# Softmax reciprocals loaded, applied and mixed earlier in the first steps of an attention and feed-forward kernel

## The chip, the core and the metric

The kernel runs on one core of a Trainium2 chip. The metric is the device time of one launch in microseconds (us). Before the change the median of three runs is 909.43 us (909.01 to 910.25).

## What is computed

Softcapped attention for 8 batches of 12 heads (448 positions, 64 wide), and a gated channel mixing on its output, all in float32:

```python
scores = cap * np.tanh(scale * q @ k.T / cap)          # cap 30, scale 1/8
attn = exp(scores - max) / (sum + 1e-9)
x = (attn @ v)                                          # 8 x 448 x 768 over all heads
x_prev = x shifted by one position
xk = mu_k * x + (1 - mu_k) * x_prev
xr = mu_r * x + (1 - mu_r) * x_prev
v = np.maximum(xk @ w_k, 0.0) ** 2 @ w_v
out = v / (1 + exp(-(xr @ w_r)))
```

## The kernel before

Two heads of a batch are a pair; there are 48 pairs, and the program is a row of steps i = 0, 1, 2, ..., one per pair, software-pipelined over several steps. Each step is written as a string of operation names (`STEP_0` for steps 0 to 5, `STEP_6`, `STEP_7`, then `EVEN_6` and `ODD_6` in turn for steps 8 to 13, and `EVEN` and `ODD` behind them), and the loop in `step` issues the operations in the order of the string. That order is the order on each engine; engines meet only through semaphores. No scheduler reorders anything.

What step i does for which pair:

- `S0` to `S3`: TensorE computes the scores of pair i, transposed (keys on the partitions), into PSUM (tile `s`, two buffers). `tanh` and `exp` (L265, L278, ScalarE) turn them into `p`. Operands are split into a high and a low float32r part, so each score product takes three matmuls.
- `red` (L308, VectorE): sums of exponentials of pair i into `r1`; `gather` (L314, four DMAs on SyncE's queue) brings those of pair i-1 to 32 partitions; `recip` (L318 to L325, four small VectorE instructions) makes their reciprocals; `rec_store` (L328) writes them to DRAM and `rec_load` (L337, two DMAs into the one buffer `r`) reads them back, broadcast to 64 partitions each. `rec_load` takes the last stored ones: in steps 2 to 6 it stands at a step's start and reads what the step before stored (pair i-2); from step 6 on a `rec_load` stands at the step's end, right behind `rec_store` and `load_qk` of the same step.
- `V` (L289, L299): TensorE multiplies values by `p` of pair i-1 into PSUM tile `pv` (two buffers). `norm` (L341, VectorE) multiplies `pv` of pair i-2 by `r` into `x`; `mix_old` (L351, ScalarE) and `mix_new` (L356, VectorE) form `xk`, and `mix_old` writes over `pv`. So `pv` of pair i-2 is free for `V` of pair i only when `mix_new` of pair i-2 has read it. `x_high` and `x_low` (GpSimd) split `xk` for the matmuls.
- `K` (L430): parts of the key matmul of the batch before, from the last part of step 6 on; `relu` and `k_store` take its results away.
- The weights arrive as 64-bit numbers and are taken apart on the way: one piece is loaded per step (`weight_load`, L463, 384 KB at first, 768 KB in steps 5 to 8, whose issue stands behind `gather` and `load_v`), `weight_abs` (ScalarE), five VectorE instructions issued by `f` (L499 to L508), `weight_sum` (GpSimd: sum L515 and high part L100). For the four 768 KB pieces the low part is a subtraction of its own, `weight_low` (L531, an instruction of L110), at the start of the next step on VectorE: `lo = sq - hi`.

All DMAs named here are issued by SyncE in program order, and one that waits holds up those behind it.

Of the kernel before, what the change touches and what calls it, by code (L numbers as in the profile page):

```python
# [60 lines left out]
K exp2 red2 weight_rest weight_sum relu k_store prep K prep K relu k_store prep  # L61
weight_abs load_qk rec_load quad_load tail_open weight_store"""
EVEN = ODD.replace("V S2", "V S3 S2").replace(" red3", "").replace("tanh2", "tanh3 tanh2").replace("K relu k_store prep\n", "K exp3 red3 relu k_store prep\n")
STEP_0 = """gather rec_load load_v x_store weight_load S0 S1 V0 S2 V1 S3 V2 V3 f f f f f tanh0 exp0 red0
weight_sum tanh1 exp1 weight_abs red1 recip rec_store qk_high qk_low tanh2 exp2 norm red2 tanh3 exp3 mix_old red3 mix_new x_high x_low
load_qk weight_store"""
ODD_6 = """load_v gather weight_load weight_low S0 S1 V S2 red3 f f f f f gate_new tanh0 exp0 red0 norm
weight_sum tanh1 exp1 K relu_early red1 tanh2 qk_rise relu exp2 mix_old k_store mix_new recip x_store rec_store qk_low x_high x_low gate_old
K red2 weight_rest weight_sum relu k_store K K weight_abs relu k_store load_qk rec_load weight_store"""
EVEN_6 = ODD_6.replace("V S2", "V S3 S2").replace(" red3", "").replace("tanh2 qk_rise", "tanh3 tanh2 qk_high").replace("weight_abs", "weight_abs exp3 red3")  # L70
STEP_6 = """gather rec_load load_v x_store weight_load weight_low S0 S1 V0 S2 V1 S3 V2 V3 f f f f f tanh0 exp0 red0
weight_sum tanh1 exp1 red1 recip rec_store tanh2 qk_rise exp2 norm red2 K K K K qk_low weight_abs tanh3 exp3 mix_old red3 mix_new x_high x_low
load_qk rec_load"""
STEP_7 = """gather load_v x_store weight_load weight_low S0 S1 V S2 f f f f f tanh0 exp0 red0 norm
weight_sum tanh1 exp1 K relu_early red1 tanh2 qk_rise relu exp2 mix_old k_store mix_new recip rec_store qk_low x_high x_low gate_old
# [6 lines left out]
def f(ap):  # L82
    return ap.bitcast(F32)


class Body:
# [440 lines left out]
                self.w_done.append((n, sq))  # L527
        self.w_sum = []

    def weight_low(self):  # L530
        for lo, sq, hi in self.w_low:  # L531
            self.sub("v", lo, sq, f(hi))
        self.w_low = []

    def weight_store(self):
        for n, sq in self.w_done:
            c, h = divmod(n - NWK, 2)
            self.nc.sync.dma_start(self.w_d[c, :, h * HC:(h + 1) * HC], sq)
        self.w_done = []
# [218 lines left out]
    def step(self, i, KS):  # L758
# [8 lines left out]
        pair.update(x_store=i - 3, gate_new=i - 3)  # L767
        for op in ((STEP_0, STEP_0) if i < 6 else (STEP_6, STEP_7) if i < ALONE else (EVEN_6, ODD_6) if i < REST[0] else (LAST, LAST) if NPAIR <= i < NPAIR + 2 else (EVEN, ODD))[i % 2].split():
            j = pair.get(op)
# [221 lines left out]
```

## Time and profile before

| | |
|---|---|
| median of 3 runs | 909.43 us |
| the profiled execution | 910.17 us, of which 908.4 us span from its first to its last instruction |
| busy, of the span | TensorE 97%, VectorE 80%, ScalarE 69%, GpSimd 45% |
| granted TensorE clock, mean | 0.997 |
| DMA | 170.03 MB, mean 187 GB/s |

The span divides into the attention steps and the two large products behind them. Steps are told apart here by the first tanh of each on ScalarE: step 2 begins at 21.22 us, step 3 at 31.04, step 4 at 40.27, step 5 at 48.66, step 6 at 57.00, step 7 at 68.11. TensorE is less than fully busy in the first 69 us and nearly without a gap behind that.

### The profile page before, as it was taken

The page shows a single profiled execution, that of the slowest core. Times are in us where ns is not written, and L with a number is a line of the kernel's source. Part 1 is how long each engine was busy: PE and PEld are TensorE (multiplying, and loading weights), DVE is VectorE, ACT ScalarE, POOL GpSimd, SP SyncE. Part 2 cuts the span into 40 slices and gives each one's busy share as a digit, 9 for nine tenths or more (in the row PEclk, how much of TensorE's full clock was granted, in tenths as well). Part 3 has the DMA queues.
Part 4 walks back from the last instruction along what each step waited for, and adds up shares of the span by engine and source line. Part 5 has one row for each costly group of instructions (what it writes and reads, how often), then busy time and mean ns, then how long its engine had stood idle before and what let it go on. Part 6 is the DMA issues. An engine that isn't in the chain of part 4 may idle for free.

```text
span 908.4 us, 15218 instructions
## 1 busy us (share of the span) xinstructions
PE 879.3 (97%) x5034; PEld 693.1 (76%) x5034; DVE 729.7 (80%) x1246; ACT 628.9 (69%) x907; POOL 411.0 (45%) x345
## 2 busy tenths in 40 slices
PE   6789999999999999999999999999999999999996
PEld 2236666666666666666666789999999999999996
DVE  6888996988988898888868857787887667877775
ACT  8888887887878887878877475556565535555553
POOL 5896584776776776776764200000000023443330
PEclk9999999999999999999999999999999999999999
DMA  5476746776766766666565455745445546777673
GB/s 166 152 212 185 213 153 196 198 203 190 210 191 198 220 195 203 197 199 197 173 197 178 161 190 179 233 149 170 151 154 166 169 149 189 219 219 218 217 219 108
DMA packets 123672, 170.03 MB, mean 187 GB/s; under 512 B 22592, under 2 KB 107712, under 8 KB 123584
## 3 DMA queue, kind: packets, MB, share of 16 engines
q1 hardware_dynamic: 114224, 154.10, 56.4%
q10 hardware_dynamic: 9360, 14.88, 4.4%
q8 instruction: 41, 0.67, 0.3%
q14 instruction: 47, 0.39, 0.1%
HBM read 109.91 MB, written 56.60 MB: 183 GB/s over the span
## 4 chain that ended last, share of the span: by engine, by line
PE 81%; DVE 5%; DMA 5%; ACT 5%; SPq 2%; issue 2%; POOL 0%; DVEq 0%; ACTq 0%; POOLq 0%
PE ps L633 39%; PE kps L430 21%; PE pv L289 10%; PE s L252 8%; DMA r<-rec_d 2%; ACT p L265 2%; PE pv L299 2%; PE s L245 2%; DVE r L308 2%; SPq L314 1%; DMA rqk<-qk 1%; ACT p L278 1%; DMA sq__194<-r 1%; DMA rec_d<-rs 1%; ACT wvh L748 1%
## 5 line engine op out<-in xcount | busy, mean ns | idle before, releaser
L308 DVE TRANSPOSE_TENSOR_REDUCE r<-p 128x28 f32<-128x896 f32 (+1 forms) x192 | 183.0, 975 | 16.6 <-ACT p L278 15.9
L265 ACT ACTIVATE p<-s,scl_t 128x896 f32<-128x896 f32 (+1 forms) x172 | 166.5, 980 | 37.6 <-PE s L252 26.7
L278 ACT ACTIVATE p<-p,cap_t 128x896 f32<-128x896 f32 (+1 forms) x172 | 174.9, 1023 | 8.4 <-ACT ko L437 2.5
L430 PE MATMUL kps<-xkh,wkh 128*128 128x448 f32 x372 | 141.8, 381 | 2.1 <-ACT ko L437 1.9
L430 PE MATMUL kps<-xkh,wkl 128*128 128x448 f32 x372 | 135.9, 365 | 0.6 <-POOL wkl L110 0.6
L430 PE MATMUL kps<-xkl,wkh 128*128 128x448 f32 x372 | 135.8, 365 | 0.0
L597 POOL TENSOR_TENSOR s<-src 128x384 f32<-128x384 f32 x14 | 14.3, 1020 | 266.1 <-DVE lo L618 261.8
L289 PE MATMUL pv<-p,rv 128*64 128x448 f32 x576 | 122.3, 553 | 9.7 <-DVE xk L356 9.7
L633 PE MATMUL ps<-wvh,hi 128*128 128x384 f32 x392 | 131.1, 334 | 0.4 <-DVE u L652 0.4
L633 PE MATMUL ps<-wvl,hi 128*128 128x384 f32 x392 | 131.0, 334 | 0.0
L617 ACT CAST hi<-s 128x512 fp32r<-128x512 f32 (+1 forms) x112 | 63.6, 568 | 89.5 <-PE ps L633 78.3
L618 DVE TENSOR_TENSOR lo<-s,hi 128x512 fp32r<-128x512 f32 (+1 forms) x112 | 70.6, 631 | 59.8 <-ACT hi L617 44.3
L110 POOL TENSOR_TENSOR qkl<-rqk,qkh 128x896 fp32r<-128x896 f32 x47 | 100.4, 2136 | 8.5 <-ACT qkh L104 5.0
L633 PE MATMUL ps<-wrh,hi 128*128 128x384 f32 x294 | 98.6, 335 | 0.3 <-DVE o L656 0.3
L633 PE MATMUL ps<-wrl,hi 128*128 128x384 f32 x294 | 98.5, 335 | 0.0
L617 ACT CAST hi<-src 128x512 fp32r<-128x512 f32 (+1 forms) x84 | 47.7, 567 | 62.0 <-PE ps L633 56.6
L289 PEld LDWEIGHTS pv<-p,rv 128*64 128x64 f32 x576 | 36.1, 137 | 70.3 <-issue 50.1
L430 PEld LDWEIGHTS kps<-xkh,wkh 128*128 128x128 f32 x372 | 69.7, 187 | 25.0 <-issue 14.5
L515 POOL TENSOR_TENSOR wsq<-wa,wsq 128x384 f32<-128x384 f32 (+1 forms) x40 | 54.2, 1355 | 73.9 <-DVE wsq L508 52.5
L633 PE MATMUL ps<-wvh,lo 128*128 128x384 f32 x392 | 83.7, 334 | 0.0
L430 PEld LDWEIGHTS kps<-xkl,wkh 128*128 128x128 f32 x372 | 69.8, 188 | 6.2
L252 PEld LDWEIGHTS s<-qkh 64*128 64x128 f32 x288 | 27.5, 186 | 61.6 <-issue 22.5
(111 smaller groups left out, 1807.9 us busy)
## 6 DMA issues: line engine op xcount, KB each, us to landing
rqk<-qk SPq DMA_DIRECT2D x47, 448.0 KB
k_d<-ko ACTq DMA_DIRECT2D x64, 224.0 KB
src<-k_d SPq DMA_DIRECT2D x56, 256.0 KB
rv<-v SPq DMA_DIRECT2D x48, 256.0 KB
r<-rec_d SPq DMA_DIRECT2D x96, 112.0 KB
v_d<-o SPq DMA_DIRECT2D x56, 192.0 KB
src<-x_d SPq DMA_DIRECT2D x42, 256.0 KB
vl<-v_d SPq DMA_DIRECT2D x56, 192.0 KB
```

The costliest lines, as they stand in the source:

```text
L110: {"p": self.nc.gpsimd, "v": self.nc.vector}[e].tensor_sub(*a)
L245: nc.tensor.matmul(s[HALF[(h + j) % 2], j % 2, 0:S], raw[p, S + KM:S + KC], raw[p, 0:S], start=True, stop=True)
L252: nc.tensor.matmul(s[:, (h + i) % 2, 0:S], qk[a][p, k], qk[b][p, 0:S], start=(n == 0), stop=(n == 2))
L265: self.nc.scalar.activation(p32[:, n], self.S.pop((i, g))[:, n, 0:S], AF.Tanh, scale=self.scl_t)
L278: self.nc.scalar.activation(p32, p32, AF.Exp, scale=1.0 if self.maxima else self.cap_t)
L289: nc.tensor.matmul(pv[p, 0:S], v[:, g, h, :], ph[:, (h + i) % 2, :], start=(g == 0), stop=False)
L308: self.nc.vector.tensor_reduce(out=r1[:, 0:RM].rearrange("p (x g) -> p x g", g=3)[:, :, g] if g < 3 else r1[:, RM:RC], in_=p32.rearrange(" ...
L430: nc.tensor.matmul(self.kps[fc][:, 0:S], w, m[:, dc, :], start=first, stop=last)
L515: {"p": self.nc.gpsimd, "v": self.nc.vector}[e].tensor_add(sq, f(a), sq)
L617: self.nc.scalar.copy(hi, x)
L618: self.nc.vector.tensor_sub(lo, x, f(hi))
L633: self.nc.tensor.matmul(o, a[:, c, :], w[:, c, :], start=first and k == 0, stop=last and k == len(todo) - 1, skip_group_check=True)
```

## The change

Three strings of operations and one small function change; no instruction is added or taken away.

```diff
-STEP_0 = """gather rec_load load_v x_store weight_load S0 S1 V0 S2 V1 S3 V2 V3 f f f f f tanh0 exp0 red0
-weight_sum tanh1 exp1 weight_abs red1 recip rec_store qk_high qk_low tanh2 exp2 norm red2 tanh3 exp3 mix_old red3 mix_new x_high x_low
+STEP_0 = """rec_load gather load_v x_store weight_load S0 S1 V0 S2 V1 S3 V2 V3 f f f f f tanh0 exp0 red0
+weight_sum tanh1 exp1 norm weight_abs red1 mix_old mix_new recip rec_store qk_high qk_low tanh2 exp2 red2 tanh3 exp3 red3 x_high x_low
 load_qk weight_store"""
-ODD_6 = """load_v gather weight_load weight_low S0 S1 V S2 red3 f f f f f gate_new tanh0 exp0 red0 norm
-weight_sum tanh1 exp1 K relu_early red1 tanh2 qk_rise relu exp2 mix_old k_store mix_new recip x_store rec_store qk_low x_high x_low gate_old
+ODD_6 = """load_v gather weight_load weight_tail S0 S1 V S2 red3 f f f f f gate_new tanh0 exp0 red0 norm
+weight_sum tanh1 exp1 K relu_early red1 mix_old tanh2 qk_rise mix_new relu exp2 k_store recip x_store rec_store qk_low x_high x_low gate_old
...
-STEP_6 = """gather rec_load load_v x_store weight_load weight_low S0 S1 V0 S2 V1 S3 V2 V3 f f f f f tanh0 exp0 red0
-weight_sum tanh1 exp1 red1 recip rec_store tanh2 qk_rise exp2 norm red2 K K K K qk_low weight_abs tanh3 exp3 mix_old red3 mix_new x_high x_low
+STEP_6 = """rec_load gather load_v x_store weight_load weight_low S0 S1 V0 S2 V1 S3 V2 V3 f f f f f tanh0 exp0 red0
+weight_sum tanh1 exp1 norm red1 mix_old mix_new recip rec_store tanh2 qk_rise exp2 red2 K K K K x_high x_low qk_low weight_abs tanh3 exp3 red3
 load_qk rec_load"""
...
-    def weight_low(self):
+    def weight_low(self, e="v"):
         for lo, sq, hi in self.w_low:
-            self.sub("v", lo, sq, f(hi))
+            self.sub(e, lo, sq, f(hi))
         self.w_low = []
+
+    def weight_tail(self):
+        self.weight_low("p")
```

`EVEN_6` is derived from `ODD_6` and changes with it. The four low parts of the 768 KB pieces stand in steps 8 to 11 and go to GpSimd, behind `x_low` of the step before.

On SyncE, at the start of step 2 and in the same way in steps 3 to 6, the two loads of the reciprocals and the gather of the next sums change places (`rec_d` is the reciprocals' buffer in DRAM, `sq` the gathered sums):

```order
 L328 DMA rec_d_66<-rs 28x32
 L181 DMA rqk<-qk 128x896
-L314 DMA sq__194<-r_1_198 32x98 x4
 L337 DMA r<-rec_d_66 64x448 x2
+L314 DMA sq__194<-r_1_198 32x98 x4
 L185 DMA rv<-v 128x512
 L463 DMA w_358<-wk 128x3x256
```

The loads now stand two places behind the store of the very reciprocals that they read, and the gather, the values and the weights stand behind them.

On VectorE, step 3, from the first sum on, before (L308 are the sums, L341 is `norm`, L356 `mix_new`, L318 to L325 `recip`):

```order
L308 TENSOR_REDUCE r_1_198<-p_492 128x28
L308 TENSOR_REDUCE r_1_198<-p_499 128x28
L318 TENSOR_REDUCE sq__194<-sq__194 32x2x14
L320 TENSOR_REDUCE sr_196<-sq__194 32x28
L323 RECIPROCAL sr_196<-sr_196 32x28
L325 STREAM_TRANSPOSE rs<-sr_196 32x32
L341 TENSOR_TENSOR x_163<-pv,r 128x448
L308 TENSOR_REDUCE r_1_198<-p_516 128x28
L308 TENSOR_REDUCE r_1_198<-p_521 128x14
L356 SCALAR_TENSOR_TENSOR xk<-x_163,mu_k,pv 128x448
```

and now:

```order
L308 TENSOR_REDUCE r_1_198<-p_492 128x28
L341 TENSOR_TENSOR x_163<-pv,r 128x448
L308 TENSOR_REDUCE r_1_198<-p_499 128x28
L356 SCALAR_TENSOR_TENSOR xk<-x_163,mu_k,pv 128x448
L318 TENSOR_REDUCE sq__194<-sq__194 32x2x14
L320 TENSOR_REDUCE sr_196<-sq__194 32x28
L323 RECIPROCAL sr_196<-sr_196 32x28
L325 STREAM_TRANSPOSE rs<-sr_196 32x32
L308 TENSOR_REDUCE r_1_198<-p_520 128x28
L308 TENSOR_REDUCE r_1_198<-p_524 128x14
```

`norm` and `mix_new` of pair i-2 now stand in front of the reciprocals of pair i-1 instead of behind them.

On ScalarE, step 6, from its second exponential on, before (L265 tanh, L278 exp, L104 the cast of the next queries and keys, L475 `weight_abs`, L351 `mix_old`):

```order
L278 ACTIVATE p_772<-p_772,cap_t 128x896
L265 ACTIVATE p_782<-s,scl_t 128x896
L104 CAST qkh<-rqk 128x896
L278 ACTIVATE p_782<-p_782,cap_t 128x896
L475 ACTIVATE wsq<-w_633 128x768
L265 ACTIVATE p_800<-s,scl_t 128x448
L278 ACTIVATE p_800<-p_800,cap_t 128x448
L351 ACTIVATE pv<-x_161,om_k 128x448
```

and now:

```order
L278 ACTIVATE p_772<-p_772,cap_t 128x896
L351 ACTIVATE pv<-x_161,om_k 128x448
L265 ACTIVATE p_786<-s,scl_t 128x896
L104 CAST qkh<-rqk 128x896
L278 ACTIVATE p_786<-p_786,cap_t 128x896
L475 ACTIVATE wsq<-w_633 128x768
L265 ACTIVATE p_805<-s,scl_t 128x448
L278 ACTIVATE p_805<-p_805,cap_t 128x448
```

`mix_old`, which waits for `norm`, now has the third and fourth tanh and exp of the step behind it, in step 6 the cast and the absolute value too.

## Rows read from the trace of the kernel before

**Rows 1.** Windows: from:to, length, busy of PE, PEld, DVE, ACT, POOL, clock, DMA, GB/s.

```profile
21.22:31.04 9.82, 7.39 (x42) 2.44 (x38) 7.51 (x14) 8.14 (x11) 9.16 (x8) 1.00 0.52 154
31.04:57.00 25.96, 21.83 (x114) 8.04 (x114) 24.38 (x43) 24.58 (x31) 23.30 (x23) 0.93 0.54 170
...
69.02:79.28 10.26, 10.26 (x54) 6.67 (x56) 10.02 (x15) 8.51 (x11) 7.49 (x7) 1.00 0.53 153
79.28:165.00 85.72, 83.69 (x487) 54.30 (x484) 71.45 (x115) 70.03 (x84) 52.49 (x42) 1.00 0.62 188
```

**Rows 2.** Timeline of TensorE, steps 3 and 7: start, length, instruction, [idle before <-releaser].

```profile
32.59 1.76 PE L289 MATMUL pv<-p,rv 128*64 128x448 f32 x4 [3.45 <-DVE xk L356]
...
67.51 0.37 PE L252 MATMUL s<-qkl,qkh 64*128 64x448 f32 x2
69.02 2.48 PE L289 MATMUL pv<-p,rv 128*64 128x448 f32 x12 [1.15 <-DVE xk L356]
```

**Rows 3.** Timeline of the SyncE queue, steps 1, 5 and 6.

```profile
20.24 0.42 SPq L328 DMA_DIRECT2D rec_d<-rs  x1
...
49.62 2.45 SPq L314 DMA_DIRECT2D sq__194<-r  x4
...
54.69 0.74 SPq L463 DMA_DIRECT2D w<-wk  x1
...
61.50 1.39 SPq L337 DMA_DIRECT2D r<-rec_d  x2
```

**Rows 4.** Timeline of the SyncE queue, steps 12 to 14.

```profile
124.57 0.34 SPq L328 DMA_DIRECT2D rec_d<-rs  x1
...
127.14 1.12 SPq L337 DMA_DIRECT2D r<-rec_d  x2
...
134.39 0.34 SPq L328 DMA_DIRECT2D rec_d<-rs  x1
...
136.01 1.12 SPq L337 DMA_DIRECT2D r<-rec_d  x2
...
144.83 0.34 SPq L328 DMA_DIRECT2D rec_d<-rs  x1
...
146.16 1.12 SPq L337 DMA_DIRECT2D r<-rec_d  x2
```

**Rows 5.** Timeline of VectorE, the three norms of the same stretch.

```profile
130.79 0.62 DVE L341 TENSOR_TENSOR x<-pv,r 128x448 f32<-128x448 f32 x1 [1.19 <-DMA r<-rec_d]
...
140.22 0.62 DVE L341 TENSOR_TENSOR x<-pv,r 128x448 f32<-128x448 f32 x1 [1.61 <-DMA sq__194<-r]
...
150.84 0.62 DVE L341 TENSOR_TENSOR x<-pv,r 128x448 f32<-128x448 f32 x1 [0.48 <-DMA r<-rec_d]
```

**Rows 6.** Timeline of ScalarE, step 6.

```profile
60.94 0.99 ACT L265 ACTIVATE p<-s,scl_t 128x896 f32<-128x896 f32 x1
63.74 0.94 ACT L104 CAST qkh<-rqk 128x896 fp32r<-128x896 f32 x1 [1.80 <-DMA rqk<-qk]
...
67.55 0.62 ACT L351 ACTIVATE pv<-x,om_k 128x448 f32<-128x448 f32 x1
```

**Rows 7.** Timeline of TensorE, steps 10 and 12.

```profile
102.00 2.48 PE L289 MATMUL pv<-p,rv 128*64 128x448 f32 x12 [0.84 <-DVE xk L356]
...
131.43 0.47 PE L430 MATMUL kps<-xkh,wkl 128*128 128x448 f32 x1 [0.62 <-POOL wkl L110]
```

**Rows 8.** Timeline of VectorE, steps 8 and 9.

```profile
90.24 0.68 DVE L356 SCALAR_TENSOR_TENSOR xk<-x,mu_k,pv 128x448 f32<-128x448 f32 x1 [2.83 <-ACT pv L351]
...
93.76 0.90 DVE L110 TENSOR_TENSOR wkl<-wsq,wkh 128x768 fp32r<-128x768 f32 x1
```

**Rows 9.** Timeline of GpSimd, steps 9 and 10.

```profile
98.92 1.86 POOL L515 TENSOR_TENSOR wsq<-wa,wsq 128x768 f32<-128x768 f32 x1 [6.12 <-DVE wsq L508]
...
104.37 2.24 POOL L110 TENSOR_TENSOR xkl<-xk,xkh 128x448 fp32r<-128x448 f32 x1
```

## The prediction

> **What bounds the kernel now.** I read the windows first, cut at the steps, then the timelines of the engines on whose waits the change bears. From 69.02 us on TensorE is the bound: it is busy for all of the 10.26 us to 79.28, and then for 83.69 of 85.72 us [rows 1]. What is done ahead of 69.02 counts only by when it lets TensorE begin there: with the values of pair 6 in step 7, which wait for `mix_new` (1.15 us) [rows 2]. Call that moment the start of the full stretch. Everything in the first steps is worth what it moves this start; everything in steps 8 to 13 is worth at most the gaps of TensorE there, 85.72 - 83.69 = 2.03 us.
>
> Ahead of that TensorE is not the bound. In steps 3 to 5 (25.96 us, 8.65 each) VectorE is busy for 24.38 us and ScalarE for 24.58, TensorE for 21.83 [rows 1]: two engines have almost no slack. The wait that looks worst, 3.45 us of TensorE for `mix_new` in step 3 [rows 2], lies in TensorE's slack; taking it away gives nothing by itself.
>
> **The reciprocals' round trip, which the change puts on the path.** Write store(j), load(j), norm(j) for `rec_store`, `rec_load` and `norm` of pair j. Before, norm(i-2) stood behind the reciprocals of pair i-1, so no step had to wait for a round trip through DRAM in order to make the next reciprocals. Now VectorE does norm(i-2), a sum, `mix_new`, then the reciprocals of i-1, whose store and load feed the next norm: a loop, and a step can't be shorter than one turn of it. The order norm, sum, `mix_new`, reciprocals, store, load is the one that steps 12 and 13 of the kernel before have already, so its length can be read there. From norm to the store: 130.79 to 134.39, 3.6 us [rows 4, 5]. From the store to the next norm: 124.57 to 130.79, 6.2; 134.39 to 140.22, 5.8; 144.83 to 150.84, 6.0 [rows 4, 5], each time with VectorE idle in front of the norm. In the middle one the store's landing takes 1.62 us until the load goes out and the load 4.21 until the norm. One turn is thus 3.6 + 5.8 = 9.4 us, if I take the shortest of the three, since the head has no results of the key matmul to store beside it; the parts put together at their shortest (store to load 1.33, at 144.83; load to norm 3.65, at 127.14) make 3.6 + 4.98 = 8.6, at their longest (2.57 at 124.57, 4.68 at 146.16) 10.85 [rows 4, 5]. All of these are above or at the 8.65 of a step now.
>
> **Step 2.** store(0) at 20.24 does not move [rows 3]. load(0) no longer stands behind the gather and goes at 20.24 + 1.33 = 21.6; norm(0) 4.0 later (between 3.65 and 4.68), at 25.6. Behind it 3.6 to store(1), at 29.2. **Steps 3 to 5.** norm(1) at 29.2 + 5.8 = 35.0, norm(2) at 44.4, norm(3) at 53.8. store(3) is at 53.8 - 5.8 = 48.0 and load(3) at 49.6.
>
> **Step 6.** Here a weight piece of 768 KB lies in front of store(4) in SyncE's queue. Before, the gather began at 49.62 and the weights were issued at 54.69, 5.1 later with the two loads between them [rows 3]. The same transfers in another order put the weights at 49.6 + 5.1 = 54.7. Before, load(4), which waits for store(4), went out at 61.50, 6.8 after the weights [rows 3]. I keep this distance: load(4) at 61.5, as before. The head start that the new order was to give the load is lost in this step. norm(4) 4.2 later, at 65.7, done at 66.3.
>
> What stands behind that norm is what makes it cost: ScalarE's `mix_old` 0.62, the third tanh 0.99, then from the cast's start to the end of the scores that follow, 63.74 to 67.51 + 0.37, 4.14 us (cast, exp, absolute value, tanh and the last scores, which need that tanh's buffer) [rows 2, 6]. Before, only `mix_old` (67.55) and `mix_new` stood behind the norm [rows 6], and the cast waited for its own data until 63.74, no more. Start of the full stretch: 66.3 + 0.1 (semaphores) + 0.62 + 0.99 + 4.14 = 72.1, against 69.02: **3.1 us later**. With the shortest turn (8.6) norm(1) is at 33.8 and norm(3) at 51.0, load(3) at 47.3 and the weights at 52.4, load(4) at 59.2, norm(4) at 62.9, the start at 69.3: 0.3 later. With 10.85 it is 76 and more.
>
> The Trainium skill, "DMA: Bandwidth & Descriptors", section "Queues, rings and completion order", says that on each DMA engine descriptors are consumed in ring order. By that the store can't pass the weights, which is what the 6.8 us in rows 3 look like; without it load(4) would go out 1.62 behind store(4), which is at 57.4, and the rival below in which the store isn't held up would hold.
>
> **Steps 8 to 13.** `mix_old` goes out ahead of the third tanh; the 2.83 us that `mix_new` waited for it in step 8 [rows 8] go, and VectorE gets rid of four subtractions of 0.90 [rows 8], the first of them in step 8. Of this TensorE sees the gaps alone: 0.84 for `mix_new` in step 10 and 0.62 for a low part of weights in step 12 [rows 7], which comes at the end of a chain through VectorE that is now some 3 us early, and some 0.1 more; 1.6 of the 2.03. `mix_old` ahead of the tanh costs ScalarE nothing: it runs the same instructions, and TensorE bounds it.
>
> The four subtractions cost GpSimd some 1.9 us each (an estimate from the sum of the same width, 1.86 [rows 9]). They stand where GpSimd idled, 6.12 us in step 9 [rows 9], so this is hidden. If that cover were gone, a low part would come late by up to its own 1.9 us, once, and TensorE would wait that long; below zero it can't go, since the matmuls need the low part at no earlier time than now.
>
> A rule speaks against this part. Rows 9 show GpSimd taking 2.24 us for a subtraction 448 wide beside VectorE, longer than 1.86 for one 768 wide. The Trainium skill, "SBUF — State Buffer", section "Who interferes with whom", says that GpSimd and a VectorE instruction with two SBUF inputs exclude each other for a whole instruction. By it VectorE would lose up to 1.9 per step instead of gaining 0.9; since VectorE has the 2.83 to spare, the sum stays the same.
>
> **Sum.** 910.17 (908.4 span and 1.8 around it) + 3.1 - 1.6 = 911.7 us; the median lies 0.74 below the profiled execution, so 910.9. Behind step 13 nothing moves but the shift.
>
> **Rivals.**
>
> *The loop is longer, and the time is slower.* The place is store to load in steps 3 to 6, where a weight piece stands in front of each store and a load of queries and keys in front of each load. For it: 2.57 and 4.68 did occur [rows 4, 5]. Against: never in the same turn. If each turn takes 0.7 more (10.1), load(3) is two turns' worth later, 1.4, and with it the weights and load(4); with 0.4 more from load(4) to its norm the start is at 73.9: +4.9 - 1.6 = +3.3, 912.7. It decides from a turn of some 9.55 on, where the loss passes 1.6 + 1.8 = 3.4 us. A long idle of TensorE in step 6 can add to it: before, 3.45 us of idleness [rows 2] went with a mean granted clock of 0.93 in steps 3 to 5 [rows 1], a piece of them at 1.2 GHz instead of 2.4.
>
> *The store isn't held up, and the time is faster.* If the turn is at its 8.6 and store(4) goes past the weights, store(4) is at 51.0 + 3.6 = 54.6, norm(4) at 59.6, and what binds is the cast's own data as before: 63.74 + 4.14 = 67.9, 1.1 earlier than 69.02. With 1.6 from the later steps that is 2.7 less: 906.7. For it: a store that is issued 3 us behind the weights, not 1, may find the queue drained. Against: 768 KB and 6.8 us.
>
> *The low parts come late on GpSimd.* Up to 1.9 us of TensorE waiting in steps 10 or 11: 912.8. Against: 6.12 us of idleness.
>
> **Numbers.** The likeliest case (0.48) is 910.9, its own range 909.0 to 912.6. The longer loop has 0.22, the store that isn't held up 0.22, the late low parts 0.08. A measurement of this kernel tells a change from none at about 0.2%, 1.8 us: faster is below 907.6, slower above 911.2. The likeliest case straddles the upper bound: 0.28 same, 0.18 slower, 0.02 faster. The long loop is slower 0.17, same 0.05; the free store faster 0.18, same 0.04; the late low parts slower 0.06, same 0.02. Together: faster 0.20, same 0.39, slower 0.41. The range is 907.2 to 914.6: it leaves out half of the fastest case and the tail of the long loop.
>
> **What would show it.** Right: VectorE idle for `r` in front of `norm` in steps 3 to 6; steps 4 and 5 at 9.2 to 9.6 us instead of 8.4; TensorE no longer waiting for `mix_new` in steps 3 to 6, but for ScalarE's tanh in step 6; the values of pair 6 at about 72; gaps at steps 10 and 12 gone. Wrong: a step of 8.4 us with no wait before the norm, load(4) before 60, or the start ahead of 69.0; or a wait for a low part in steps 9 to 11.

## The result, and the profile after

The changed kernel takes 917.93 us (median of six, 916.96 to 920.16), the kernel before 909.78 beside it: 1.0088 times as long, interval 1.0071 to 1.0105, some 8 us slower. I had forecast 910.9, at most 914.6.

The profiled execution takes 918.33 us, its span is 916.4. Windows of the changed kernel, cut at the same work as [rows 1] (steps 3 to 5, step 6, step 7, steps 8 and later), columns as there:

```profile
31.16:58.64 27.48, 23.58 (x120) 8.32 (x116) 24.73 (x43) 24.50 (x32) 25.44 (x25) 0.90 0.58 174
58.64:71.90 13.26, 9.36 (x49) 3.84 (x45) 9.20 (x17) 10.01 (x13) 9.43 (x9) 0.95 0.68 205
71.90:83.20 11.30, 11.30 (x57) 6.92 (x56) 9.41 (x16) 8.49 (x11) 7.45 (x6) 0.91 0.52 167
83.20:171.57 88.37, 84.37 (x487) 53.86 (x484) 70.79 (x111) 70.02 (x84) 56.68 (x45) 1.00 0.58 177
```

Three things are to be seen. Steps 3 to 5 take 27.48 us in place of 25.96, and step 6 13.26 in place of 12.02. Step 7 takes 11.30 in place of 10.26 though TensorE is busy throughout, at a mean clock of 0.91 in place of 1.00. And the last stretch has 88.37 - 84.37 = 4.00 us of TensorE's gaps where before had 2.03, the very stretch in which I had expected gaps to go.

Step 6, all engines, changed kernel:

```profile
61.56 1.12 SPq L337 DMA_DIRECT2D r<-rec_d  x2
...
65.16 0.63 DVE L341 TENSOR_TENSOR x<-pv,r 128x448 f32<-128x448 f32 x1 [2.50 <-DMA r<-rec_d]
65.82 0.64 ACT L351 ACTIVATE pv<-x,om_k 128x448 f32<-128x448 f32 x1 [3.15 <-DVE x L341]
66.40 0.99 ACT L265 ACTIVATE p<-s,scl_t 128x896 f32<-128x896 f32 x1
67.53 0.47 PE L252 MATMUL s<-qkh 64*128 64x448 f32 x2 [1.70 <-ACT p L265]
...
70.52 0.70 PE L252 MATMUL s<-qkh 64*128 64x448 f32 x2 [2.12 <-ACT p L265]
...
71.90 3.50 PE L289 MATMUL pv<-p,rv 128*64 128x448 f32 x12
```

This is the chain of the forecast: the load at 61.56, 61.50 in [rows 3], `norm` waits for it, `mix_old` for `norm`, the third tanh behind `mix_old` (it stood ahead of the cast in [rows 6], `mix_old` at 67.55), TensorE for the tanh. V of pair 6, V(6) for short (the values matmuls of step 7), starts at 71.90, 2.88 late. Its 12 matmuls then take 3.50 us, 2.48 in [rows 2].

TensorE and ScalarE of the changed kernel, 103 to 135 us:

```profile
102.98 0.64 ACT L351 ACTIVATE pv<-x,om_k 128x448 f32<-128x448 f32 x1 [2.25 <-DVE x L341]
...
109.96 0.99 ACT L265 ACTIVATE p<-s,scl_t 128x896 f32<-128x896 f32 x1
111.00 0.47 PE L252 MATMUL s<-qkh 64*128 64x448 f32 x2 [0.99 <-ACT p L265]
...
115.29 0.64 ACT L351 ACTIVATE pv<-x,om_k 128x448 f32<-128x448 f32 x1 [3.27 <-DVE x L341]
...
122.15 0.47 PE L252 MATMUL s<-qkh 64*128 64x448 f32 x2 [1.05 <-ACT p L265]
...
135.09 0.47 PE L252 MATMUL s<-qkh 64*128 64x448 f32 x2 [0.99 <-ACT p L265]
```

The gaps of [rows 7] are gone, and new ones stand in their place, all for ScalarE's tanh: `mix_old` waits 2.25 and 3.27 us for `norm`, with the tanh queued behind it. The delay travels along ScalarE's queue: the tanh that ends TensorE's wait at 111.00 is the second one of the next step (109.96), and from `mix_old` at 102.98 to it ScalarE idles only once, for 0.40 us.

### The profile page after: what moved, and what is told of

Same layout as the page of the kernel before. It is cut to its first block, busy times and chain, and to the rows that moved or that the text cites. A ratio compares the mean times of both kernels' runs of the same rounds, so it can differ in the third digit from the quotient of the medians.

```text
span 916.4 us, 15212 instructions
## 1 busy us (share of the span) xinstructions
PE 886.3 (97%) x5034; PEld 694.7 (76%) x5034; DVE 727.4 (79%) x1242; ACT 628.1 (69%) x907; POOL 417.1 (46%) x349
## 4 chain that ended last, share of the span: by engine, by line
PE 78%; DMA 7%; ACT 6%; DVE 5%; issue 2%; SPq 1%; POOL 0%; DVEq 0%; ACTq 0%
PE ps L636 39%; PE kps L430 20%; PE pv L289 9%; PE s L252 8%; DMA r<-rec_d 3%; ACT p L265 2%; DMA rec_d<-rs 2%; PE pv L299 1%; DMA sq__194<-r 1%; PE s L245 1%; ACT p L278 1%; DVE r L308 1%; SPq L314 1%; ACT ko L437 1%; SPq L337 1%
## 5 line engine op out<-in xcount | busy, mean ns | idle before, releaser
L308 DVE TRANSPOSE_TENSOR_REDUCE r<-p 128x28 f32<-128x896 f32 (+1 forms) x192 | 183.4, 976 | 25.2 <-ACT p L278 24.3
L265 ACT ACTIVATE p<-s,scl_t 128x896 f32<-128x896 f32 (+1 forms) x172 | 166.3, 979 | 36.6 <-PE s L252 26.0
L278 ACT ACTIVATE p<-p,cap_t 128x896 f32<-128x896 f32 (+1 forms) x172 | 174.9, 1024 | 9.0 <-ACT ko L437 2.4
L289 PE MATMUL pv<-p,rv 128*64 128x448 f32 x576 | 124.7, 562 | 1.0 <-DVE xk L356 1.0
L430 PEld LDWEIGHTS kps<-xkh,wkh 128*128 128x128 f32 x372 | 69.7, 187 | 25.6 <-issue 14.5
L252 PEld LDWEIGHTS s<-qkh 64*128 64x128 f32 x288 | 28.0, 189 | 74.9 <-issue 26.9
L252 PE MATMUL s<-qkh 64*128 64x448 f32 x288 | 65.8, 452 | 18.2 <-ACT p L265 13.7
```

The source lines that it names most:

```text
L252: nc.tensor.matmul(s[:, (h + i) % 2, 0:S], qk[a][p, k], qk[b][p, 0:S], start=(n == 0), stop=(n == 2))
L265: self.nc.scalar.activation(p32[:, n], self.S.pop((i, g))[:, n, 0:S], AF.Tanh, scale=self.scl_t)
L278: self.nc.scalar.activation(p32, p32, AF.Exp, scale=1.0 if self.maxima else self.cap_t)
L289: nc.tensor.matmul(pv[p, 0:S], v[:, g, h, :], ph[:, (h + i) % 2, :], start=(g == 0), stop=False)
L308: self.nc.vector.tensor_reduce(out=r1[:, 0:RM].rearrange("p (x g) -> p x g", g=3)[:, :, g] if g < 3 else r1[:, RM:RC], in_=p32.rearrange(" ...
L430: nc.tensor.matmul(self.kps[fc][:, 0:S], w, m[:, dc, :], start=first, stop=last)
```

## Experiments

TensorE runs the same matmuls in the same order in all of these kernels, so a *shift* can be read: the start of a matmul less the start of the same one in the first trace of before. Columns: at V of pair 6 (69.02 in before), behind it (84.66), behind step 13 (145.36) and behind the attention (588.78).

| trace | V(6) | 84.66 | 145.36 | 588.78 |
|---|---|---|---|---|
| changed kernel | 2.88 | 3.92 | 6.56 | 8.50 |
| e5, changed again | 3.11 | 4.87 | 7.00 | 9.44 |
| e17, a third time | 3.62 | 4.75 | 7.01 | 7.13 |
| e16, before again | -0.34 | -0.33 | 1.26 | 1.29 |
| e1, head alone | 2.56 | 4.21 | 4.46 | 3.99 |
| e2, steps 8 to 13 alone | -2.00 | -1.99 | 1.73 | 1.50 |
| e3, sooner mixing alone | -1.78 | -1.78 | 0.51 | 0.93 |
| e4, low parts alone | 0.15 | 1.72 | 2.75 | 2.23 |
| e14, head and mixing | 3.03 | 5.16 | 7.38 | 7.67 |
| e6, reciprocals first | 10.33 | 12.00 | 12.00 | 14.87 |
| e7, mixing late in head | 1.62 | 3.09 | 3.10 | 3.47 |
| e11, loads first alone | 3.53 | 4.94 | 4.96 | 6.10 |
| e15, gather first | 14.52 | 16.74 | 16.86 | 16.45 |
| e12, head, weights sooner | 2.98 | 3.00 | 3.39 | 4.18 |
| e10, mixing behind tanh | 0.25 | 0.27 | 0.45 | 0.46 |
| e8, step 8 alone | 0.29 | 0.30 | -0.57 | -0.22 |
| e13, e8, weights sooner | -1.28 | -1.26 | -2.26 | 0.52 |
| e18, e13 again | -1.03 | -1.01 | -1.50 | -0.89 |

Kernels with the head of before reach V(6) 2 us early to 0.3 late, and a half clock (a stretch in which the granted clock is 1.2 GHz and not 2.4) can fall anywhere in the head or, in e16, at 103.8 to 107.3 us. In e9 below, which is the kernel before up to step 20, the shift is -1.37 at V(6) and -0.21 behind step 13, with no half clock between. So a shift is good to 1 to 2 us where single executions are compared; what is said below rests on waits that recur, and on the times. A time in us that stands beside a ratio is that ratio's.

One column is the clock's: from V(6) to 84.66 the shift grows by 1.0 to 2.2 us in ten traces, and in these ten the granted clock is 1.2 GHz within V(6) or just behind it; in the others it grows by 0.02 at most. Nine of the ten have a late head (all such traces but e12), one (e4) has the head of before.

**Where is the loss?** Four kernels, each with one part of the change.

e1 has `STEP_0` and `STEP_6` of the changed kernel, the rest of before. 

> The head's edits alone (STEP_0 and STEP_6 new, steps 8 to 13 as before). Theory A, two independent losses: the head's own shift stays, V of pair 6 starts near 71.9 us and TensorE is 3.9 us behind from there on, of which 1.0 is the half clock (1.2 GHz) after its wait in step 6; steps 9 to 13 give nothing back and lose nothing, so 913.5 to 915 us, and the shift at the end is the shift at 90 us, within 1 us. Theory B, the head's shift itself makes the later losses, because the later loads and stores meet other work: steps 9 to 13 and the end of the stretch lose as in the changed kernel, 917 to 918. A tail loss near 500 us that comes with the head alone (915.5 to 916.5) would put that part on the shift.

Measured: 913.0 us, 1.0049 times before (1.0033 to 1.0064), 4.5 us, half a microsecond under what A said. Nothing more is lost between 84.66 and 145.36 (4.21, 4.46).

e2 has the rest of the change and the head of before. 

> Steps 8 to 13 alone as changed (mixing sooner, low parts on GpSimd), the head as before. Theory A: the early mix_old waits on ScalarE for its norm and holds the third tanh, for whose score buffers TensorE then waits, 1 us at each of three or four places, less the 0.8 and 0.6 us of waits that go: TensorE is 2 to 2.7 us behind after step 13, so 911.5 to 912.5. Theory B: without the head's shift the norm comes in time and the steps gain the 1.6 us that were forecast: 908. My forecast's own term says 907.8.

Measured: 911.74 us, 1.0031 (1.0015 to 1.0046), 2.8 us. The two losses add up to 7.3 of the 8 by the ratios, each good to some 1.4 us, and to 5.9 of 8.2 by the medians: theory A, two independent places, with up to 2 us left over (the loss behind 500 us, below). Theory B falls, and with it the 1.6 us that I had counted as a gain.

e3: in `ODD_6` and `EVEN_6` only the mixing moves.

```diff
-... red1 tanh2 qk_rise relu exp2 mix_old k_store mix_new recip ...
+... red1 mix_old tanh2 qk_rise mix_new relu exp2 k_store recip ...
```

> Only the order of mixing in steps 8 to 13; the low parts stay on VectorE. Theory A (the place of mix_old ahead of the third tanh makes the loss): TensorE loses 1 to 3 us over steps 9 to 13, 910.5 to 912.5. Theory C (the moved subtractions make it, by slowing VectorE beside GpSimd, so that the norm is late): without them mix_old waits no longer than the tanh would anyway, 908.5 to 910.

Measured: 912.36 us, 1.0033 (1.0019 to 1.0047). ScalarE's `mix_old` and TensorE in this kernel:

```profile
84.84 0.64 ACT L351 ACTIVATE pv<-x,om_k 128x448 f32<-128x448 f32 x1
...
97.38 0.64 ACT L351 ACTIVATE pv<-x,om_k 128x448 f32<-128x448 f32 x1 [2.34 <-DVE x L341]
...
105.40 0.47 PE L252 MATMUL s<-qkh 64*128 64x448 f32 x2 [0.99 <-ACT p L265]
```

No low part has moved, and the loss is there: A, not C. In step 8 `mix_old` finds its `norm` done; in steps 9 to 12 it waits, 2.34 here, where before, with tanh and exp ahead of it (at 100.40 us), it waited 0.92. TensorE's three waits of about 1 us for a tanh recur in all six traces that mix sooner in all of steps 8 to 13 (three of the changed kernel, e2, e3, e14).

e4: only the low parts move.

```diff
-ODD_6 = """load_v gather weight_load weight_low S0 ...
+ODD_6 = """load_v gather weight_load weight_tail S0 ...
```

> Only the low parts on GpSimd in steps 8 to 13, mixing in the order of before. Theory A: the slowed weight chain of VectorE has slack, TensorE's 0.62 us wait for the low part in step 13 goes, 908.5 to 910.5. Theory C: VectorE's instructions beside the moved subtraction take 1.8 and 2.1 us in place of 1.0 and 0.6, the norm and the probabilities behind them are late, and TensorE is 1.5 to 2.5 us behind: 911 to 912.

Measured: 912.26 us, 1.0024 (1.0005 to 1.0042). GpSimd, VectorE and TensorE:

```profile
106.54 2.16 POOL L110 TENSOR_TENSOR wkl<-wsq,wkh 128x768 fp32r<-128x768 f32 x1
...
107.04 2.08 DVE L502 TENSOR_SCALAR wa<-wsq 128x768 uint32<-128x768 uint32 x1
...
119.45 1.93 POOL L110 TENSOR_TENSOR wkl<-wsq,wkh 128x768 fp32r<-128x768 f32 x1
119.75 2.06 DVE L504 SCALAR_TENSOR_TENSOR wa<-w,wa 128x384 uint32<-128x384 uint32 x1
...
121.44 0.47 PE L430 MATMUL kps<-xkh,wkl 128*128 128x448 f32 x1 [1.45 <-POOL wkl L110]
```

My rival of the late low parts, given 0.08, is what happens here: TensorE waits 1.45 us for one. The traces of the changed kernel do not have this wait; that their matmuls are late already would explain it, but was not tested. The VectorE instructions beside the subtraction take 2.08 and 2.06 us; alone they take 0.56 each (in before). The time is near C's, but not for its reason: of this trace's 2.75 us behind step 13, 1.57 are the half clock at V(6), ahead of the first moved subtraction at 80.50 us, and only 1.03 arise between 84.66 and 145.36. C's path, through `norm` and the probabilities, is not what the trace shows either.

**Is it the place of `mix_old`?** e10 puts it behind the third tanh, still ahead of the exp:

```diff
-... tanh2 qk_rise relu exp2 mix_old k_store mix_new recip ...
+... tanh2 mix_old qk_rise mix_new relu exp2 k_store recip ...
```

> Steps 8 to 13 mix sooner than before, but right behind the third tanh (and, in even steps, the fourth) in place of ahead of it; the low parts stay on VectorE, the head is that of before. Theory A, the hold: TensorE's score buffers are freed in time, the jumps of +1.1, +1.0 and +1.6 us at 106, 115 and 127 us go and the waits at 102 and 131 us that the sooner mixing took out (0.8 and 0.9) stay out, 908 to 909.5. Rival: the probabilities behind mix_old are late instead and hold TensorE's value matmuls as long, 911 to 912.5.

Measured: 909.97 us, 0.9989 (0.9973 to 1.0005). By the times the loss is gone; the trace still has a part of it:

```profile
100.09 0.64 ACT L351 ACTIVATE pv<-x,om_k 128x448 f32<-128x448 f32 x1 [2.30 <-DVE x L341]
...
107.23 0.48 PE L252 MATMUL s<-qkh 64*128 64x448 f32 x2 [0.99 <-ACT p L265]
```

The wait is as long as ahead of the tanh; what is late behind it is the exp, the `relu` that empties the key matmul's PSUM, and the tanh of the next step. The jump at 115 is gone, that at 106 is not, and at 128.96 a wait of 0.64 us stands in place of 0.99. So what stands behind the waiting instruction matters: with the third tanh ahead of it the times show no loss. The shifts alone would not tell, since e3 reached V(6) 1.78 early and both are 0.5 late behind step 13.

e8 keeps the one step in which nothing waits, step 8.

```diff
+EVEN_8 = EVEN_6.replace("tanh3 tanh2 qk_high relu exp2 mix_old k_store mix_new",
+                        "mix_old tanh3 tanh2 qk_high mix_new relu exp2 k_store")
-... (EVEN_6, ODD_6) if i < REST[0] ...
+... (EVEN_8 if i == 8 else EVEN_6, ODD_6) if i < REST[0] ...
```

> Only step 8 mixes sooner; steps 9 to 13 and the head as before. In the trace with mixing sooner in all of them, step 8's mix_old found its norm done (no wait) and VectorE lost its 2.8 us wait for it. Theory A: TensorE's 0.84 us wait of before at 102 us for xk goes, and nothing is held: 0.8 us faster, 908.3 to 909.3, with the gain to be read in TensorE's shift between 95 and 150 us, since the times scatter by more. If early mixing is harmful in itself, the shift grows there.

Measured: 908.43 us, 0.9985 (0.9972 to 0.9999). ScalarE, VectorE and TensorE, to set beside [rows 7, 8] (line numbers are one higher in this kernel):

```profile
86.92 0.63 ACT L352 ACTIVATE pv<-x,om_k 128x448 f32<-128x448 f32 x1
87.67 0.68 DVE L357 SCALAR_TENSOR_TENSOR xk<-x,mu_k,pv 128x448 f32<-128x448 f32 x1
...
101.58 2.48 PE L290 MATMUL pv<-p,rv 128*64 128x448 f32 x12
```

The waits of 2.83 and 0.84 us are both gone and none has come: the 0.84 of [rows 7] was lost in step 8, two steps ahead of where it shows. This is the fastest of the kernels, ahead of before and of the changed one; its gain is near the limit of what can be told.

**What makes the head late?** e7 keeps the loads and `norm` early and puts the mixing back to the end of the step (against the changed kernel's `STEP_0`; `STEP_6` likewise).

```diff
-... norm weight_abs red1 mix_old mix_new recip rec_store ... exp3 red3 x_high ...
+... norm weight_abs red1 recip rec_store ... exp3 mix_old red3 mix_new x_high ...
```

> The head with the loads ahead of the gather and the normalisation ahead of the reciprocals, as changed, but with mixing where it was, behind the fourth tanh. The loop is then norm, reciprocal, store, load, without the 1.6 us of mixing: 7.8 us where the shortest step of before is 8.6. Theory A: no loss, V of pair 6 at 68 to 70 us, 908.5 to 910. A loss of 2 us or more all the same would say that the normalisation's place, not the length of the loop, is what costs.

Measured: 912.6 us, 1.0024 (1.0011 to 1.0036), 2.2 us of the head's 4.5: theory A falls. The forecast's loop is cut short here; the period is not. SyncE's weights (L463), loads (L337) and a store (L328) in steps 3 to 5 of e7, and VectorE's `norm`:

```profile
35.03 0.59 DVE L341 TENSOR_TENSOR x<-pv,r 128x448 f32<-128x448 f32 x1
35.98 1.44 SPq L463 DMA_DIRECT2D w<-wk  x1
40.96 1.12 SPq L337 DMA_DIRECT2D r<-rec_d  x2
44.48 0.62 DVE L341 TENSOR_TENSOR x<-pv,r 128x448 f32<-128x448 f32 x1 [1.16 <-DMA r<-rec_d]
45.81 0.38 SPq L463 DMA_DIRECT2D w<-wk  x1
47.48 0.34 SPq L328 DMA_DIRECT2D rec_d<-rs  x1
...
50.44 1.12 SPq L337 DMA_DIRECT2D r<-rec_d  x2
53.99 0.62 DVE L341 TENSOR_TENSOR x<-pv,r 128x448 f32<-128x448 f32 x1 [1.19 <-DMA r<-rec_d]
```

and the same in the changed kernel:

```profile
35.48 0.63 DVE L341 TENSOR_TENSOR x<-pv,r 128x448 f32<-128x448 f32 x1 [0.30 <-DMA r<-rec_d]
36.52 0.38 SPq L463 DMA_DIRECT2D w<-wk  x1
41.11 1.12 SPq L337 DMA_DIRECT2D r<-rec_d  x2
44.77 0.63 DVE L341 TENSOR_TENSOR x<-pv,r 128x448 f32<-128x448 f32 x1 [0.84 <-DMA r<-rec_d]
45.96 0.38 SPq L463 DMA_DIRECT2D w<-wk  x1
48.37 0.34 SPq L328 DMA_DIRECT2D rec_d<-rs  x1
...
50.58 1.12 SPq L337 DMA_DIRECT2D r<-rec_d  x2
54.21 0.62 DVE L341 TENSOR_TENSOR x<-pv,r 128x448 f32<-128x448 f32 x1 [0.99 <-DMA r<-rec_d]
```

Mixing is out of the loop in e7, which takes 0.6 us out of the way from norm to store (44.48 to 47.48 in place of 44.77 to 48.37; the 1.6 of my expectation did not lie on it), yet the norms are 9.45 and 9.51 us apart, 9.29 and 9.44 in the changed kernel. Common to both is SyncE's queue: from a load 4.85 us to the weights issued behind it (41.11 to 45.96, 40.96 to 45.81), then 4.59 to 4.98 until the next load can go, which waits for a store issued behind those weights. 4.85 + 4.6 = 9.45. The store of e7 is issued 1.67 us behind the weights (45.81 to 47.48), that of the changed kernel 2.41 (45.96 to 48.37), and the load goes 4.63 and 4.62 behind them all the same. The DMA packets kept in the traces show why: the store's last packet ends 0.02 us behind the last of those weights in e7 and 0.03 behind it in the changed kernel (49.88 and 50.07 us), and the same 0.02 and 0.03 behind the 768 KB of step 5 (61.20 and 60.89). So in these steps the store lands with the weights ahead of it, whether it is issued sooner or later. Before, the gather's 2.44 us of issuing stood between the store and the load, while the store landed; now they stand behind the load's wait.

e11 moves only the two loads, in `STEP_0` and `STEP_6`.

```diff
-gather rec_load load_v ...
+rec_load gather load_v ...
```

> Only the two loads of the reciprocals ahead of the gather in the head; VectorE and ScalarE in the order of before. Before's normalisation stands behind the reciprocals and two sums and does not wait for the load in steps 5 and 6, so the sooner load gives nothing there. Theory A (the loss of the head needs the normalisation ahead of the reciprocals): 909 to 910.5, V of pair 6 within 1 us of 69. Rival Q (SP's queue: the loads wait for the store's landing, and the gather behind them is late): V of pair 6 at 70.5 us or later, 911.5 to 912.5, as with the normalisation moved.

Measured: 915.01 us, 1.0055 (1.0036 to 1.0073), 5.0 us: rival Q by V(6), 3.53 late, and more than its time. SyncE and VectorE, steps 5 and 6:

```profile
55.92 2.71 SPq L463 DMA_DIRECT2D w<-wk  x1
63.43 1.12 SPq L337 DMA_DIRECT2D r<-rec_d  x2
64.64 2.44 SPq L314 DMA_DIRECT2D sq__194<-r  x4
...
68.41 0.49 DVE L318 TENSOR_REDUCE sq__194<-sq__194 32x28 f32<-32x336 f32 x1 [4.25 <-DMA sq__194<-r]
```

The load waits for its store until 63.43 and the gather, which went at 57.96 in before, waits behind it; the reciprocals wait 4.25 us for the sums. So the place of the loads alone costs as much as the whole head (e1): a load that has to wait was put in front of a gather that could go sooner. What is late for it here is the sums, since VectorE's order is that of before; in the changed kernel it is the load itself.

e15 is e1 with these two changed back (`gather rec_load`). 

> The head as changed except that the gather stands ahead of the loads again on SP (as before); normalisation and mixing stay ahead of the reciprocals. Loads ahead of the gather alone cost 5.5 us. If that is what costs in the changed head too (theory Q), V of pair 6 returns to within 1 us of 69 and the time is 909 to 910.5. If the changed head has its own cause (theory A: mix_old ahead of the third tanh waits for the normalisation, which waits for a load whose store stands behind 768 KB of weights, wherever the gather is), V of pair 6 stays 2 us late or more, 912 to 914.

Measured: 926.74 us, 1.0183 (1.0159 to 1.0207), worse than either theory said. (The 5.5 us that I gave the loads there are 5.0 by e11's ratio.) `norm` (VectorE):

```profile
40.84 0.63 DVE L341 TENSOR_TENSOR x<-pv,r 128x448 f32<-128x448 f32 x1 [3.01 <-DMA r<-rec_d]
...
52.34 0.63 DVE L341 TENSOR_TENSOR x<-pv,r 128x448 f32<-128x448 f32 x1 [3.04 <-DMA r<-rec_d]
```

By the order of the strings each load now stands behind a gather, which needs sums, which need the tanh that `mix_old` holds; the turn is 11.5 us. With `norm` early the loads must be early too, and both then cost: none of the parts of the head's change that were tried (e7, e11, e15, e6) is as fast as before.

e6 has the loads first and the reciprocals ahead of `norm` again (against the changed kernel).

```diff
-... norm weight_abs red1 mix_old mix_new recip rec_store ...
+... weight_abs red1 recip rec_store norm mix_old mix_new ...
```

> The head as changed, but with the reciprocals and their store ahead of the normalisation again (mixing follows the normalisation, before the third tanh). Theory A, the loop: the store no longer waits for the normalisation, the loop norm, mix, reciprocal, store, load of 9.4 us per step is cut, the last norm of step 6 comes near 62 us in place of 65.4, V of pair 6 starts within 1 us of before's 69.0, and the time is 909 to 910.5. Rival H, the hold: it is mix_old ahead of the third tanh, waiting on ScalarE for its norm, that holds TensorE in the head as it does in steps 9 to 12, whatever sets the norm; then V of pair 6 is still 2 us late or more and the time is 912 to 914.

Measured: 922.19 us, 1.0127 (1.0105 to 1.0150). `mix_old` in step 6 of e6:

```profile
73.84 0.64 ACT L351 ACTIVATE pv<-x,om_k 128x448 f32<-128x448 f32 x1 [4.11 <-DVE x L341]
```

Rival H, and more than its 2 us: the held tanh makes the sums late, these the reciprocals, behind which `norm` stands: norms at 39.61, 50.46 and 61.30, a turn of 10.85 us. I had the direction of A wrong.

e12 is e1 with the weights of step 5 sooner.

```diff
+STEP_5 = STEP_0.replace("load_v x_store weight_load", "weight_load load_v x_store")
```

> The head as changed, steps 8 to 13 as before, and the 768 KB of weights of step 5 issued ahead of that step's values and x store, 1.2 to 1.3 us sooner (54.3 in place of 55.6 us in the changed kernel). Theory W: the load of step 6 waits for a store of 3.5 KB that lands only when the 768 KB are through, and the norm, mix_old and the third tanh wait for that load; then load, norm and V of pair 6 all come about 1.2 us sooner than with the head alone (load 60.4, norm 64, V 70.4 to 70.7), and the time is 911.5 to 912.5. Rival: the load waits for the length of the loop (norm, mix, reciprocal, store), which the weights do not touch; load and norm stay at 61.5 and 65.3, 913 to 914.

Measured: 912.93 us, 1.0034 (1.0020 to 1.0048). The weights went at 55.04, only 0.69 sooner than in e1, and the load at 61.45, 0.36 sooner; V(6) was not. This could not decide it: the values and the x store that the weights passed now stand between them and the store, whose packets end at 60.75, 0.99 behind the weights' last.

e13 does the same on e8. 

> The kernel before with step 8 alone mixing sooner and with the same earlier issue of the 768 KB in step 5. In before, the sums of pair 5 land at 64.4 us, behind the same weights, and VectorE waits 1.65 us for them ahead of the chain to V of pair 6, for which TensorE waits 1.15. Theory W: the sums land 1.3 us sooner, TensorE's 1.15 us wait at 69.02 goes, and with the 1.0 us of step 8 the shift at 150 us is 2 us to the good: 907 to 908.2. If the chain has another limit, it is the time of step 8 alone, 908.4 to 909.

Measured: 910.39 us, 1.0009 (0.9997 to 1.0021). The weights went at 53.40, the sums were there at 62.74 without a wait, TensorE's 1.15 us wait shrank to 0.24, and V(6) started 1.28 early. That is what theory W says, but no evidence for it: e2 and e3, with the weights in their old place, began V(6) 2.00 and 1.78 early. The time is not W's; behind 500 us the lead was lost.

**The loss behind 500 us.** In two traces of the changed kernel TensorE loses 1.9 and 2.4 us there, in two waits: one for `mix_new` behind a late gather, and one for ScalarE to empty the key matmul's PSUM (1.31 us at 537.05 in the first). VectorE and TensorE of the first, at the first wait:

```profile
511.58 0.49 DVE L318 TENSOR_REDUCE sq__194<-sq__194 32x28 f32<-32x336 f32 x1 [1.52 <-DMA sq__194<-r]
513.64 2.48 PE L289 MATMUL pv<-p,rv 128*64 128x448 f32 x12 [0.99 <-DVE xk L356]
```

e5 is the changed kernel unaltered, and so is e17 below. 

> The changed kernel once more, for the 1.1 and 1.2 us that its trace lost near 506 and 530 us, which the head alone and the middle alone did not lose. If these belong to the change, TensorE's shift against before grows by about 2 us between 480 and 580 us again, and the time is 917 to 919. If they are chance of the transfers there, the shift at 580 us is within 0.5 us of that at 480 us, which is 6 to 8 us, and the time is 915.5 to 917.5.

Measured: 918.49 us, and the loss is there again (7.00 to 9.44).

e9 pushes everything back.

```diff
+for _ in range(34 if (i, g) == (20, 0) else 0):
+    nc.tensor.matmul(s[:, 0, 0:S], qk[0][HALF[0], k], qk[0][HALF[0], 0:S], start=True, stop=True)
```

> The kernel before with 34 idle matmuls of 448 columns (overwritten by the first real one, nothing else changed) ahead of the scores of pair 20, near 200 us: all of the work behind them is pushed back by 34 x 0.24 = 8 us, with no order changed. Both profiles of the changed kernel lost 1.9 and 2.5 us near 506 to 545 us, where the head alone and the middle alone lost nothing. If such a loss goes with any shift of 6 us or more (the one with 12 us had it too), it shows here: the shift at 600 us is 10 us and the time 919 to 920. If it comes from what the changed kernel does, the shift at 600 us stays 8 us, 917 to 918.

Measured: 916.08 us; the idle matmuls took 0.20 each, a shift of 6.9 us, and it was 6.32 behind the attention. In this one execution a shift alone lost nothing.

e14 is e1 and e3 together. 

> The changed kernel with the low parts of the weights on VectorE as before: the head and the sooner mixing of steps 8 to 13. If the two places add up, 4.2 to 4.5 us of the head and 2.3 of the middle: shift 6.5 to 7 us at 440 us, and 915.5 to 917. If the loss of 1.9 to 2.5 us near 506 to 545 us that both traces of the changed kernel showed needs the head and the sooner mixing together, it shows here (917.5 to 919); if it needs the low parts on GpSimd, it does not.

Measured: 917.15 us, 1.0079 (1.0053 to 1.0105), without the loss (7.38, 7.67). So head and mixing carry nearly the whole time of the changed kernel.

e16 is the kernel before. 

> The kernel before once more, for how far one execution's trace differs from another: the same program began V of pair 6 at 67.0 to 69.2 us in four kernels with the head of before. I expect V of pair 6 within 2 us of 69.0 and the shift behind it unchanged to 600 us within 0.5 us; a jump of 1 to 3 us between 500 and 545 us here would say that the loss there is chance of an execution.

Measured: 911.18 us; V(6) as expected, nothing lost behind 500. Not as expected are the 1.6 us lost in steps 9 to 13, where a half clock fell.

e17: 

> The changed kernel a third time. If the 1.9 and 2.5 us near 506 to 545 us belong to it, they are here again (shift at 600 us 8.5 to 9.5); if they are chance, the shift at 600 us is within 0.5 us of that at 440 us.

Measured: 917.32 us, no loss there (7.01, 7.13).

e18 is e13 unaltered. 

> The kernel with step 8 mixing sooner and the 768 KB issued earlier once more. Its first trace was 2.3 us ahead at 150 us and lost 2.8 us between 500 and 580 us, though it is not behind before at all. If that loss belongs to a program, it comes again; if it is chance of an execution, this one keeps its lead and takes about 907.5 us.

Measured: 909.43 us, 0.6 us lost where the first had lost 2.8. The same program loses there in one execution and hardly in another: it is no fixed part of the change. In this trace `mix_old` of step 8 waits 0.26 us for `norm`, so that step is not free of the wait in every execution. Why the gather behind 500 us is late in some executions stays open.

## Why the prediction was wrong

| step | forecast | three traces of the changed kernel |
|---|---|---|
| load(4) | 61.5 | 61.56 in the first |
| norm(0) to norm(4) | 25.6, 35.0, 44.4, 53.8, 65.7 | 26.72, 35.48, 44.77, 54.21, 65.16 in the first |
| start of the full stretch | +3.1 | +2.9, +3.1, +3.6 |
| clock in V(6) | only beside a rival | +1.0, +1.8, +1.1 |
| steps 8 to 13 | -1.6 | +2.6, +2.1, +2.3 |
| behind step 13 | 0 | +1.9, +2.4, +0.1 |

**The step that failed is "`mix_old` ahead of the tanh costs ScalarE nothing: it runs the same instructions, and TensorE bounds it."** It runs the same instructions, but idles in another place: in step 9 2.3 us with the tanh still to do, in place of 0.9 with it done. TensorE bounds the stretch only as long as the tanh frees its score buffers in time. I had said this of step 6 and did not ask it of steps 9 to 13, where the trace already had `norm` late. In place of the 1.6 us of gain the sooner mixing alone made the kernel 1.0033 times as long (e3), and behind the third tanh it cost nothing that the times show (e10). In the traces of the changed kernel -1.6 became +2.1 to +2.6: some 4 us of the 7 that I missed. The rest is the clock (1.0 to 1.8) and, in two traces of three, the loss behind 500 us (1.9 and 2.4). The two gaps did go, as forecast; e8 shows that the one in step 10 can be had by itself.

The low parts: I wrote that VectorE has the 2.83 to spare, so that the rule of the shared port changes nothing. It has them in step 8 only. e4 shows VectorE's slowed instructions in steps 10 and 11, and TensorE's wait of 1.45 us behind them in step 11.

The clock: I named it only as what could come on top of a rival. In the three traces the granted clock is at 1.2 GHz at 70.6 to 74.0, 68.8 to 75.7 and 68.1 to 74.9 us, across V(6), after a step 6 in which TensorE idled 13.26 - 9.36 = 3.9 us in the first. Its idleness in step 6 alone does not settle it, since before idled 12.02 - 8.49 = 3.5 us there and stayed at full clock (columns as in [rows 1]):

```profile
57.00:69.02 12.02, 8.49 (x47) 3.49 (x45) 10.00 (x18) 10.12 (x13) 9.84 (x9) 1.00 0.79 229
```

In two traces of before it is low elsewhere; e4, with the head of before, has it here too. It is a measured term of 1 to 1.8 us that goes with a late head in nine traces of ten and with the head of before in one of ten (e9, e13 and e18 among them); what starts it is not shown.

The head: start and period came out, from a chain that is only half right, and in part by luck. The period is that of SyncE's queue, not of norm, mixing and reciprocals (e7, e11); I had seen the store behind the weights in step 5 alone, and it stands there in every step. The 5.8 us from store to norm that I chose as the shortest has the gather and not the load as its releaser in [rows 5]. Two errors cancel in load(4): load(3) and the weights of step 5 went 1.0 and 0.9 us later than forecast (50.58 and 55.61), and the load 5.95 us behind those weights, not 6.8. That the weights hold the store is what its packets say; taking the weights away was not tried. The rule on ring order that I weighed for step 6 (the Trainium skill, "DMA: Bandwidth & Descriptors", section "Queues, rings and completion order") fits them: in steps 3 to 5 of the changed kernel and of e7 the load goes 4.6 to 6.4 us after the weights ahead of its store, the longest behind the 768 KB.

## What to carry to other kernels

Before an instruction that waits is moved forward in an in-order queue, list what will stand behind it and who needs that: here it was the tanh behind `mix_old` and the gather behind the loads that the engines needed. Ask it step by step, since the same move costs nothing in the step whose input is early (e8) and a microsecond in the next. A forecast that meets its landmarks may still have the wrong loop: cut the loop and see whether its period goes.

## What the runs showed of the hardware

A VectorE `TENSOR_SCALAR` of 128x768 with one SBUF input took 2.08 us beside a GpSimd subtraction, and 0.56 alone. I had taken the rule for instructions with two inputs; the Trainium skill, "SBUF — State Buffer", section "Who interferes with whom", also lists `tensor_scalar` among those that can take the shared pair, and these traces agree.

A store of 3.5 KB issued behind weights of 384 or 768 KB on the same queue ended 0.02 to 0.13 us behind them in steps 3 to 5 of the changed kernel and of e7, also where it was issued 0.7 us sooner.

The same program differed by up to 1.6 us between two traces over steps 8 to 13 (e16) and by 2.3 us behind 500 us (changed kernel), while its median is good to a few tenths of a per cent.
